# A retention-plus-MLP kernel: two loads moved behind two turns, the last product cut 192 and 64, and the first q fetched from two queues

## The chip, the cores and the metric

The kernel runs on one core of a Trainium2 chip. Its time is device microseconds of one execution; the median of three runs stands for it. Inside the core, TensorE (PE) multiplies, VectorE (DVE), ScalarE (ACT) and GpSimd (POOL) do elementwise work and copies, and SyncE (SP), ACT and POOL start DMAs.

## The reference

A retention recurrence over 4 batches, 8 heads, 768 steps and head size 64 gives `y`; its rows, heads side by side, are the 3072 tokens of an MLP with 512 inputs and 2048 hidden units and the activation `h * tanh(softplus(h))` (Mish).

```python
state = gamma * state + k_t v_t^T          # per head, gamma = 1 - 2^-(5+h)
y_t   = scale * q_t state
x     = y.transpose(0, 2, 1, 3).reshape(3072, 512)
h     = x @ w_in                            # 512 x 2048
out   = mish(h) @ w_out                     # 2048 x 512
```

## The kernel before

The recurrence is done in chunks of 128 steps: inside a chunk a masked score product `k q` and its product with `v`, across chunks a 64x64 state per head. There are 24 chunks. They are gathered into blocks of tokens for the MLP: block 0 holds four chunks, and blocks 1 to 10 two chunks each. For a block of two chunks both matrix products are done by a seven-product scheme on 2x2 parts (sums of parts are formed on DVE, seven products run on PE, and the results are added up), so their accumulators are copied out part by part.

The order of all work is written by hand. `g1_seven` runs the first product in the order of the string `ORDER`; `seven` runs the second. Between the products stand named steps (`at1`, `m1`, `m2`, ...), and `steps_of_first(1)` and `steps_of(blk)` say what each does for the chunks of later blocks: load q and v (`load_to`, on SP), bring k (`bring_k`, on POOL's queue), scale q and v to half precision on POOL (`cast_q`, line 414, `cast_v`, line 431), turn q and k of a chunk by a DMA transpose (`turn_by_dma`, line 443, on SP), score (`scores_two`, line 509), mask, outer products and states. `store` and `store_due` send finished rows out on SP. Each engine and each queue takes its work in the order in which the program lists it.

In block 1, step `at5` stores two tiles and calls `load_to(a + 4)`, which loads q and v of chunk 11; then step `m5` turns chunk 8, and step `m2` turns chunk 9. Both turns' results are read by `scores_and_outer(9)` in block 2, which scores chunks 8 and 9 in one group of 32 small products.

At the start, `load_first_q` fetches q of the first four chunks (tile `qfirst`) in two parts of four heads, both on SP, and then k, v and the weights follow on SP. The small table of decay factors, `qvs`, comes on ACT's queue. DVE scales the first half of `qfirst` (line 257) and PE turns it (line 264); DVE and POOL share the second half. Ahead of the first turn PE does filler products on constants (`spin_wide`, `spin`, lines 457 and 452).

At the end, for the last block, `seven` does after six products: `s(4) b(1,1)` into `pe`, whose sum goes out at once (half of the columns of one row tile, 128 KB, on SP); `s(3) tm(3)` into `px`, from which two sums fill the other row tile (256 KB, on ACT's queue); and `a(0,1) b(1,0)` in two pieces of 128 columns, whose sums fill the other half of the first row tile (128 KB, on SP).

Of the kernel before, what the change touches and what calls it, by code (L numbers as in the profile page):

```python
# [10 lines left out]
FP32 = mybir.dt.float32  # L11
AF = mybir.ActivationFunctionType
ALU = mybir.AluOpType
# [3 lines left out]
def kernel(  # L17
# [9 lines left out]
    nc = tc.nc  # L27
    B, H, S, D = q.shape
    d_model, d_ff = moe_w_in.shape
    P = 128  # L30
# [4 lines left out]
    TB = 512  # L35
    CPB = TB // C
# [3 lines left out]
    first = [sum(BLOCKS[:i]) for i in range(len(BLOCKS))]  # L40
# [17 lines left out]
    def toks(c):  # L58
        return slice(c * HB, (c + 1) * HB)
# [16 lines left out]

    ctx.enter_context(tc.manual_schedule())

    qvs = cpool.tile([P, (2 + CPB + R) * H], FP32, name="qvs")
    nc.scalar.dma_start(qvs, nc.inline_tensor(qvs_np, name="qvs_c").ap())  # L80
    qs, vs = qvs[:, :H], qvs[:, H:2 * H]
# [20 lines left out]
    for c in range(2):  # L102
        t = tri_half[toks(c)]
# [6 lines left out]
    for c in range(2):  # L110
        t = tri_first[c * HB:(c + 1) * HB]
# [114 lines left out]
    def rows(blk, i):  # L226
        r = out[first[blk] * P:(first[blk] + 2) * P]
        if blk <= FIRST:
            return r[i * P:(i + 1) * P]
        return r.rearrange("(n c t) d -> c t n d", n=2, c=2)[i]  # L230
# [8 lines left out]
            store(1)  # L239

    def load_first_q():

        qf = wstage.tile([P, H, CPB, D], FP32, name="qfirst", tag="wt", bufs=4)
        for a in range(0, H, H // 2):
            nc.sync.dma_start(
                qf[:, a:a + H // 2],
                q[0, a:a + H // 2, :TB].rearrange("h (p r) d -> p h r d", r=CPB))
        return qf  # L250

    def turn_first_q(qf, half, shared=False):
        a, n = half * (H // 2), H // 2
# [672 lines left out]

    def seven(blk, steps, last, rest):
        n, hf = NFB // 2, d_model // 2
        parts = 2 if last else 1
        wide = hf // parts  # L930
        px, pe = [mmps.tile([P, hf], FP32, name="o_ps", tag="mm") for _ in range(2)]
        osb = [op.tile([P, d_model], FP32, name="osb", tag="osb") for _ in range(2)]

        def a(i, j):
            return lambda f: gts[blk, j * n + f][:, i * P:(i + 1) * P]

        def b(i, j):
# [8 lines left out]
        def pieces(o_ps):  # L946
            if isinstance(o_ps, list):
                return [(t, slice(i * wide, i * wide + wide)) for i, t in enumerate(o_ps)]
            return [(o_ps, slice(0, hf))]

        def mm(o_ps, x, w, first=False, then=None):
            for t, c in pieces(o_ps):
                for f in range(n):
                    nc.tensor.matmul(  # L954
                        t, x(f), w(f)[:, c], start=first and f == 0, stop=f == n - 1,
                        skip_group_check=True)
                if then:
                    then(t, c)

        def snap(o_ps):  # L960
            x = op.tile([P, hf], FP32, name="snap", tag="snap", bufs=4)
            for t, c in pieces(o_ps):
                nc.scalar.copy(x[:, c], t)  # L963
            return x

        def store_now(queue, i, c):
            queue.dma_start(rows(blk, i)[..., c], osb[i][:, c])

        def done(i, j, o_ps, plus=None):
            dst = osb[i][:, j * hf:(j + 1) * hf]  # L970
            for t, c in pieces(o_ps):
                if plus is None:
                    nc.scalar.copy(dst[:, c], t)
                else:
                    nc.vector.tensor_tensor(dst[:, c], t, plus[:, c], op=ALU.add)  # L975

        def step(name):
            for fn, *args in steps.get(name, ()):
                fn(*args)

        mm(px, a(0, 0), b(0, 0), True)
        m1 = snap(px)
        step("g7")
        step("m1")
        if last:
            pz = mmps.tile([P, hf], FP32, name="o_ps", tag="mm")
            mm(pz, a(1, 1), tm(4), True)
            z = snap(pz)
        rest()
        pb = [mmps.tile([P, wide], FP32, name="o_ps", tag="mm") for _ in range(parts)]  # L990
        mm(pe, s(1), tm(1), True)
        m5 = snap(pe)
        step("m5")
        mm(px, s(2), tm(2))
        u2 = snap(px)
        step("m6")
        if last:
            mm(pe, s(4), b(1, 1))
            done(0, 1, pe, u2)
            store_now(nc.sync, 0, slice(hf, d_model))  # L1000
            mm(px, s(3), tm(3))
            done(1, 1, px, m5)
            done(1, 0, px, z)
            store_now(nc.scalar, 1, slice(0, d_model))
            mm(pb, a(0, 1), b(1, 0), True)
            done(0, 0, pb, m1)
            store_now(nc.sync, 0, slice(0, hf))
            return
        mm(pb, a(0, 1), b(1, 0), True)
        done(0, 0, pb[0], m1)  # L1010
        step("m2")
        mm(px, s(3), tm(3))
        done(1, 1, px, m5)
        step("m7")
        if blk > TURN:
            mm(px, a(1, 1), tm(4))
            done(1, 0, px)
        mm(pe, s(4), b(1, 1))
        if blk > TURN:
            step("m3")  # L1020
        done(0, 1, pe, u2)
        if blk <= TURN:
            step("m3")
            mm(px, a(1, 1), tm(4))
            done(1, 0, px)
        step("m4")
        for i in range(2):
            stores.append((1 + i, rows(blk, i), osb[i]))
# [28 lines left out]
                start=bp == 0, stop=bp == NBP - 1, skip_group_check=True)  # L1057

    def first_block():
        qf = load_first_q()  # L1060
        for s in range(2):
            for nm in "kv":
                for half in range(2):
# [348 lines left out]
```

## Time and profile before

| | |
|---|---|
| median of 3 runs | 192.39 us (192.24 to 194.35) |
| profiled execution | 191.71 us |
| its span in the profile | 189.8 us |
| PE busy | 183.3 us, 97% |
| DVE busy | 156.7 us, 83% |
| ACT busy | 126.0 us, 66% |
| POOL busy | 94.7 us, 50% |
| read from and written to HBM | 27.30 MB and 6.29 MB |

Rows of a timeline read: start in us, length in us, engine, line, operation, what is written <- what is read, partitions x elements, count, and in brackets how long the engine was idle before and what ended it. `SPq` and `ACTq` rows are issues of DMAs, whose landing comes later. A row of several stretches gives, for each, its length, the busy time of each engine with the number of instructions, the TensorE clock, the DMA share and GB/s. Rows of the DMA view end with the size in KB and the median us from issue to landing. In the chain of waits, each row is a piece of the path that ended last: start, length, what.

### The profile page before, as it was taken

To read this page: it belongs to the slowest core of one execution; us is meant where nothing else is said; L and a number is where in the kernel's file an instruction comes from. 1 tells how busy PE (TensorE), PEld (TensorE's weight loads), DVE (VectorE), ACT (ScalarE), POOL (GpSimd) and SP (SyncE) were. 2 spreads that over 40 slices of the span, in tenths; PEclk is the share of its full clock that TensorE was granted. 3 is DMA by queue.
4 is the path that set the end of the run, shared out by engine and by line. 5 is a ranking of instruction groups with operands and counts; after the bars stand their busy time and mean duration, and the time that the engine had idled before them with its cause. 6 is when DMAs were issued, how large, how long until landed. Compare 5 with 4: busy or idle time off the path is not lost.

```text
span 189.8 us, 7746 instructions
## 1 busy us (share of the span) xinstructions
PE 183.3 (97%) x3298; PEld 156.9 (83%) x3298; DVE 156.7 (83%) x330; ACT 126.0 (66%) x244; POOL 94.7 (50%) x135
## 2 busy tenths in 40 slices
PE   6989999999999999999999999999999999999992
PEld 2667546875988988988988988988988988989981
DVE  3997899889899698797897897797897897796662
ACT  3362699463893983894883883983884974975960
POOL 6570205696767937934934935915925923000000
PEclk9999999999999999999999999999999999999999
DMA  4999999999999999999996996996997953300203
GB/s 165 351 369 406 405 406 279 269 217 147 186 195 281 193 264 217 175 192 170 176 184 148 159 176 196 207 233 40 196 205 106 155 152 60 114 3 12 102 0 111
DMA packets 95521, 36.17 MB, mean 191 GB/s; under 512 B 82560, under 2 KB 88960, under 8 KB 95488
## 3 DMA queue, kind: packets, MB, share of 16 engines
q1 hardware_dynamic: 74112, 32.78, 73.7%
q0 software_dynamic: 21088, 2.62, 21.7%
q8 instruction: 25, 0.41, 0.9%
q10 hardware_dynamic: 288, 0.30, 0.4%
q14 instruction: 8, 0.07, 0.1%
HBM read 27.30 MB, written 6.29 MB: 177 GB/s over the span
## 4 chain that ended last, share of the span: by engine, by line
PE 94%; DVE 3%; issue 1%; POOL 0%; ACT 0%; POOLq 0%; DVEq 0%
PE h_ps L818 34%; PE o_ps L954 32%; PE h_ps L687 6%; PE o_ps L1207 5%; PE at L457 2%; PE h_ps L1055 2%; PE o_ps L1267 2%; PE y_ps L542 2%; PE at L509 2%; PE u_ps L495 2%; DVE am L329 2%; PE y_ps L553 2%; PE t_ps L264 1%; DVE osb L975 1%; PE at L322 0%
## 5 line engine op out<-in xcount | busy, mean ns | idle before, releaser
L838 DVE TENSOR_TENSOR hsum<-h_ps,hsnap 128x512 f32<-128x512 f32 x60 | 38.6, 685 | 9.7 <-ACT hsnap L828 6.8
L828 ACT COPY hsnap<-h_ps 128x512 f32<-128x512 f32 x60 | 32.1, 589 | 10.0 <-PE h_ps L818 9.7
L818 PEld LDWEIGHTS <-wsum 128*128 128x128 f16 x640 | 36.2, 98 | 0.2
L833 ACT ACTIVATE g<-hsum 128x512 f16<-128x512 f32 x60 | 34.6, 642 | 0.6 <-DVE hsum L838 0.2
L954 PEld LDWEIGHTS <-gsum 128*128 128x128 f16 x320 | 30.4, 98 | 3.7
L818 PE MATMUL h_ps<-xsum,wsum 128*128 128x128 f16 x480 | 30.2, 219 | 0.0
L954 PE MATMUL o_ps<-tmat,gsum 128*128 128x256 f16 x240 | 29.5, 273 | 0.0
L818 PEld LDWEIGHTS <-win 128*128 128x128 f16 x480 | 28.2, 98 | 0.9
L426 POOL DMA_DIRECT2D qk<-in_k_dram x36 | 27.6, 781 | 0.0
L954 PEld LDWEIGHTS <-g 128*128 128x128 f16 x248 | 22.7, 98 | 2.5
L414 POOL TENSOR_TENSOR qk<-qf,qvs 128x512 f16<-128x512 f32 x20 | 21.5, 1077 | 0.2 <-issue 0.2
L431 POOL TENSOR_TENSOR v<-vf,qvs 128x512 f16<-128x512 f32 x20 | 21.2, 1085 | 0.0
L954 PE MATMUL o_ps<-wout,g 128*128 128x256 f16 (+1 forms) x168 | 20.8, 267 | 0.0
L818 PE MATMUL h_ps<-xt,win 128*128 128x128 f16 x320 | 19.6, 219 | 0.0
L603 POOL TENSOR_TENSOR stc<-suc,gcv 128x256 f16<-128x256 f32 x15 | 9.9, 663 | 15.7 <-DVE suc L598 15.7
L560 ACT COPY hsum<-y_ps 128x512 f32<-128x512 f32 x9 | 5.3, 585 | 18.4 <-PE y_ps L553 18.4
L975 DVE TENSOR_TENSOR osb<-o_ps,snap 128x256 f32<-128x256 f32 (+1 forms) x32 | 13.0, 413 | 5.0 <-PE o_ps L954 2.5
L439 POOL COPY gate<-gsum 128x1 f16<-128x1 f16 x10 | 1.8, 185 | 26.8 <-DVE gsum L925 26.8
L963 ACT COPY snap<-o_ps 128x256 f32<-128x256 f32 x31 | 11.4, 371 | 5.5 <-PE o_ps L954 5.3
L818 PE MATMUL h_ps<-xsum,win 128*128 128x128 f16 x160 | 12.3, 220 | 0.0
L818 PE MATMUL h_ps<-xt,wsum 128*128 128x128 f16 x160 | 12.2, 219 | 0.0
L833 ACT ACTIVATE g<-h_ps 128x512 f16<-128x512 f32 x20 | 12.0, 598 | 0.0
(142 smaller groups left out, 310.6 us busy)
## 6 DMA issues: line engine op xcount, KB each, us to landing
vf<-in_v_dram SPq DMA_DIRECT2D x24, 256.0 KB, 6.0
out_dram<-osb SPq DMA_DIRECT2D x22, 256.0 KB, 3.5
qf<-in_q_dram SPq DMA_DIRECT2D x20, 256.0 KB, 4.9
wi<-in_moe_w_in_dram SPq DMA_DIRECT2D x3, 1024.0 KB, 10.5
wt<-in_moe_w_out_dram SPq DMA_DIRECT2D x3, 1024.0 KB, 9.3
qk<-in_k_dram POOLq DMA_DIRECT2D x36, 64.0 KB, 4.7
qfirst<-in_q_dram SPq DMA_DIRECT2D x2, 512.0 KB, 4.3
kf<-in_k_dram SPq DMA_DIRECT2D x4, 256.0 KB, 5.0
```

Of the source, the lines that this page charges most:

```text
L414: nc.gpsimd.tensor_tensor(by_head(g, room16(g)[0]), by_head(0, loaded[g][0]), f.broadcast_to((P, 2, HP, D)), op=ALU.mult)
L426: nc.gpsimd.dma_start(room16(g)[1][:, x::2], src[:, HP * x:HP * x + HP])
L431: nc.gpsimd.tensor_tensor(room16(g)[2], loaded[g][2], vs.unsqueeze(2).broadcast_to((P, H, D)), op=ALU.mult)
L603: by.tensor_tensor(stcs[g], sus.pop(g), decay, op=ALU.mult)
L687: nc.tensor.matmul(h_ps[:, j], win(s, f, bp), xt(blk, bp), start=(bp == 0), stop=(bp == NBP - 1))
L818: nc.tensor.matmul(h_ps[g][:, f], w(g, f, d), x(d), start=first and f == 0 and d == 0, stop=d == n - 1, skip_group_check=True)
L828: nc.scalar.copy(x, h_ps)
L833: nc.scalar.activation(gt[:, fb:fb + FPS, j * P:(j + 1) * P], h, AF.Mish, scale=inv_boost3)
L838: nc.vector.tensor_tensor(h, h_ps, x, op=ALU.add)
L954: nc.tensor.matmul(t, x(f), w(f)[:, c], start=first and f == 0, stop=f == n - 1, skip_group_check=True)
L963: nc.scalar.copy(x[:, c], t)
L975: nc.vector.tensor_tensor(dst[:, c], t, plus[:, c], op=ALU.add)
```

## The change

Three edits, independent of each other. The first q is loaded at the very beginning of the program in three parts: heads 2 and 3 on ACT's queue ahead of `qvs`, heads 0 and 1 on SP, then heads 4 to 7 on SP. In block 1, `load_to(a + 4)` moves from step `at5` to step `m2`, behind the turn of chunk 9. In the last block, `a(0,1) b(1,0)` is cut into 192 columns ahead of the last two products and 64 columns behind them, these two change places, and the stores become 256 KB on ACT, 224 KB and 32 KB on SP. On PE, DVE, ACT and POOL nothing else moves; on SP all else keeps its order.

```diff
+    qf = wstage.tile([P, H, CPB, D], FP32, name="qfirst", tag="wt", bufs=4)
+    for queue, h0, n in ((nc.scalar, 2, 2), (nc.sync, 0, 2), (nc.sync, 4, 4)):
+        queue.dma_start(
+            qf[:, h0:h0 + n],
+            q[0, h0:h0 + n, :TB].rearrange("h (p r) d -> p h r d", r=CPB))
     qvs = cpool.tile([P, (2 + CPB + R) * H], FP32, name="qvs")
     nc.scalar.dma_start(qvs, nc.inline_tensor(qvs_np, name="qvs_c").ap())
...
-    def load_first_q():
-
-        qf = wstage.tile([P, H, CPB, D], FP32, name="qfirst", tag="wt", bufs=4)
-        for a in range(0, H, H // 2):
-            nc.sync.dma_start(
-                qf[:, a:a + H // 2],
-                q[0, a:a + H // 2, :TB].rearrange("h (p r) d -> p h r d", r=CPB))
-        return qf
...
     def seven(blk, steps, last, rest):
         n, hf = NFB // 2, d_model // 2
-        parts = 2 if last else 1
-        wide = hf // parts
+        near = D
...
         if last:
-            mm(pe, s(4), b(1, 1))
-            done(0, 1, pe, u2)
-            store_now(nc.sync, 0, slice(hf, d_model))
+            def left(c):
+                pb = mmps.tile([P, c.stop - c.start], FP32, name="o_ps", tag="mm")
+                mm(pb, a(0, 1), b(1, 0), True, c)
+                done(0, 0, pb, m1, c)
+
+            left(slice(near, hf))
             mm(px, s(3), tm(3))
             done(1, 1, px, m5)
             done(1, 0, px, z)
             store_now(nc.scalar, 1, slice(0, d_model))
-            mm(pb, a(0, 1), b(1, 0), True)
-            done(0, 0, pb, m1)
-            store_now(nc.sync, 0, slice(0, hf))
+            mm(pe, s(4), b(1, 1))
+            done(0, 1, pe, u2)
+            store_now(nc.sync, 0, slice(near, d_model))
+            left(slice(0, near))
+            store_now(nc.sync, 0, slice(0, near))
             return
...
     def first_block():
-        qf = load_first_q()
...
-            "at5": [(store, 2), (load_to, a + 4), (sums_a, blk, A)],
+            "at5": [(store, 2), (sums_a, blk, A)],
...
             "m2": [(sums_c, blk), (gate_s, blk), (cast_q, a + 1), (turn_by_dma, a + 1),
-                   (store, 2)],
+                   (load_to, a + 4), (store, 2)],
```

More of the change, by code (lines that the diff above doesn't have):

```diff
@@ L944, in tm, with mm @@
             return lambda f: tmats[(i - 1) // 2][:, (i - 1) % 2, f]
[L946 to L958, printed above, removed]
+        def mm(o_ps, x, w, first=False, c=slice(0, hf)):
+            for f in range(n):
+                nc.tensor.matmul(
+                    o_ps, x(f), w(f)[:, c], start=first and f == 0, stop=f == n - 1,
+                    skip_group_check=True)
         def snap(o_ps):
             x = op.tile([P, hf], FP32, name="snap", tag="snap", bufs=4)
-            for t, c in pieces(o_ps):
-                nc.scalar.copy(x[:, c], t)
+            nc.scalar.copy(x, o_ps)
             return x
@@ L967, in store_now, with done @@
             queue.dma_start(rows(blk, i)[..., c], osb[i][:, c])
[L969 to L975, printed above, removed]
+        def done(i, j, o_ps, plus=None, c=slice(0, hf)):
+            dst = osb[i][:, j * hf:(j + 1) * hf][:, c]
+            if plus is None:
+                nc.scalar.copy(dst, o_ps)
+            else:
+                nc.vector.tensor_tensor(dst, o_ps, plus[:, c], op=ALU.add)
         def step(name):
@@ L989, in seven @@
         rest()
-        pb = [mmps.tile([P, wide], FP32, name="o_ps", tag="mm") for _ in range(parts)]
+        if not last:
+            pb = mmps.tile([P, hf], FP32, name="o_ps", tag="mm")
         mm(pe, s(1), tm(1), True)
@@ L1004, in seven @@
             store_now(nc.scalar, 1, slice(0, d_model))
-            mm(pb, a(0, 1), b(1, 0), True)
-            done(0, 0, pb, m1)
-            store_now(nc.sync, 0, slice(0, hf))
+            mm(pe, s(4), b(1, 1))
[3 more added lines that the diff above has]
+            store_now(nc.sync, 0, slice(0, near))
             return
         mm(pb, a(0, 1), b(1, 0), True)
-        done(0, 0, pb[0], m1)
+        done(0, 0, pb, m1)
         step("m2")
```

## The prediction

> **What bounds the kernel now.** I read the page first, then the chain of work that ended last, then the stretches of the three places that the change touches. The page's head and its chain shares say that TensorE is the bound nearly everywhere:
>
> ```profile
> span 189.8 us, 7746 instructions
> PE 183.3 (97%) x3298; PEld 156.9 (83%) x3298; DVE 156.7 (83%) x330; ACT 126.0 (66%) x244; POOL 94.7 (50%) x135
> ...
> PE 94%; DVE 3%; issue 1%; POOL 0%; ACT 0%; POOLq 0%; DVEq 0%
> ```
>
> The profiled execution took 191.71 us: a span of 189.8 and 1.9 around it. The three runs have their median at 192.39, 0.68 above it. So a load, a store or a turn matters only where PE waits for it, at the start before PE is saturated, or after PE's last product. The chain in order of time gives those places (start, length, what):
>
> ```profile
> 6.50 0.85 PE t_ps L264 x8
> ...
> 8.45 0.24 PE t_ps L307 x4
> ...
> 68.64 0.13 PE at L509 x16
> 68.77 0.02 issue
> 68.78 0.32 PE at L509 x16
> ...
> 185.30 1.19 DVE osb L975 x4
> ```
>
> The reader is to see a chain that is PE almost without a break, one seam at 68.77 in the middle of a group of score products, and a tail that is DVE and then the store.
>
> **The moved loads.** The seam first. The busy time of line 509 alone, for the 32 score products of two successive blocks:
>
> ```profile
> 68.46:69.03 0.57, 0.55 (x32) 0.40 (x32) 1.00 1.35 212
> 82.77:83.34 0.57, 0.37 (x32) 0.26 (x32) 1.00 1.65 196
> ```
>
> The same 32 products stretch over 0.55 us in the block that scores chunks 8 and 9 and over 0.37 in the next: PE loses about 0.18 us between chunk 8's 16 and chunk 9's. The issue queues before it, and then the landing of the second transpose alone:
>
> ```profile
> 57.81 1.03 POOL L414 TENSOR_TENSOR qk<-qf,qvs 128x512 f16<-128x512 f32 x1
> 58.76 0.45 SPq L155 DMA_DIRECT2D qf<-in_q_dram  x1
> 59.26 0.83 SPq L155 DMA_DIRECT2D vf<-in_v_dram  x1
> 59.66 1.04 POOL L414 TENSOR_TENSOR qk<-qf,qvs 128x512 f16<-128x512 f32 x1
> 60.27 2.98 SPq L443 DMA_TRANSPOSE qkt<-qk  x1
> 63.42 1.23 SPq L443 DMA_TRANSPOSE qkt<-qk  x1
> ```
>
> ```profile
> DMA to landing us min/median/max: 5.3/5.3/5.3
> ```
>
> 63.42 + 5.3 = 68.7: chunk 9's turn lands just when PE goes on at 68.78. That turn is what PE waits for. The change takes two issues (0.45 + 0.83 us of SP, 256 KB each) from before the two turns to behind the second. The first turn's q is scaled at 57.81 + 1.03 = 58.84, so it can be issued at about 58.9 instead of 60.27, 1.4 us earlier. The second, whose q is ready at 60.70, stays behind the first turn's 2.98 us of issue and goes at about 62.0 instead of 63.42. Its data also no longer stands behind 512 KB of chunk 11 in the queue. It lands at 67.4 at the latest, with 1.2 us to spare before 68.6. The gain in this execution is therefore the stall and nothing more: -0.18 us. Since the landing sits on the very edge, an execution in which it is later loses more there, and the median is 0.68 above the profiled one; bounds for the runs are 0.18 to 0.18 + 0.68 = 0.86, and I take 0.4, between the two and nearer the one row that shows it.
>
> What is late next: chunk 11's v and q. They are issued at about 63.3 and 63.8. The page's medians from issue to landing, and the first use, the scaling of v:
>
> ```profile
> vf<-in_v_dram SPq DMA_DIRECT2D x24, 256.0 KB, 6.0
> ...
> qf<-in_q_dram SPq DMA_DIRECT2D x20, 256.0 KB, 4.9
> ```
>
> ```profile
> 71.86 1.03 POOL L431 TENSOR_TENSOR v<-vf,qvs 128x512 f16<-128x512 f32 x1
> ```
>
> So both are there by 69.8, and 2 us are left. Behind the moved loads on SP stand two stores and chunk 12's loads; SP does the same total work up to there, and no engine waits for the stores. I cost the delay at nothing; without that margin, POOL's scaling and the state products behind it would slip one for one.
>
> **The first q.** Today two 512 KB parts come one behind the other on SP, and the small table `qvs` (32 KB) on ACT's queue. Afterwards ACT's queue brings heads 2 and 3 and only then `qvs`; SP brings heads 0 and 1 and then heads 4 to 7. The second half keeps its place: the same bytes are ahead of it.
>
> ```profile
> 0.74 1.00 SPq L247 DMA_DIRECT2D qfirst<-in_q_dram  x2
> 4.69 2.02 DVE L257 TENSOR_TENSOR qfirst<-qfirst,qvs 128x1024 f16<-128x1024 f32 x2 [1.80 <-DMA qfirst<-in_q_dram]
> 5.44 1.06 PE L452 MATMUL at<-ident 128*128 128x512 f16 x2
> 5.97 0.10 PEld L264 LDWEIGHTS <-qfirst 128*128 128x128 f16 x1 [0.37 <-DVE qfirst L257]
> 6.14 1.49 POOL L257 TENSOR_TENSOR qfirst<-qfirst,qvs 128x512 f16<-128x512 f32 x1 [1.98 <-DMA qfirst<-in_q_dram]
> 6.29 1.06 PE L264 MATMUL t_ps<-ident,qfirst 128*128 128x128 f16 x8
> ```
>
> DVE indeed waits 1.80 us for the first half. But PE is then in its filler products on `tri` and `ident`, which stand ahead of the transposes in its own order. The two on `ident` start at 5.44 and the transposes follow at 6.29 without a gap, while their weights could be loaded at 5.97. An earlier q moves DVE's cast, not the transposes: gain 0 in this execution. A later q costs only beyond the slack of about 0.2 us (5.97 against 6.29, less one weight load of 0.10). How fast the first bytes come (0.2 us a slice, from the start):
>
> ```profile
> GB/s 0 0 0 0 0 0 0 0 9 146 33 41 148 68 164 374 333 389 389 389 379 379 394 374 389 389 374 351 353 340 356 338 348 340 346 341 340 353 343 343
> ```
>
> From 1.8 to 3.0 the queue runs at about 100 GB/s, and from 3.0 at 370. If that slow stretch belongs to one queue, two of them shorten it; at best the whole 1.2 us less 0.3 for its bytes, 0.9. If it belongs to the engines, nothing changes, and `qvs`, now behind 256 KB, lands with the q instead of ahead of it. [...] I take 0, with -0.3 to +1.1 as bounds (both under the rivals).
>
> **The last product.** The order s(4)·b, s(3)·t, then 128 and 128 columns becomes 192 columns, s(3)·t, s(4)·b, then 64 columns; the stores, 128 KB early, 256 and 128 KB late, become 256 KB on ACT, 224 KB and 32 KB on SP, all late.
>
> ```profile
> 183.35 1.04 PE L954 MATMUL o_ps<-wout,gsum 128*128 128x256 f16 x8
> 183.55 0.37 ACT L963 COPY snap<-o_ps 128x256 f32<-128x256 f32 x1 [0.50 <-PE o_ps L954]
> 184.23 1.04 PE L954 MATMUL o_ps<-tmat,gsum 128*128 128x256 f16 x8
> 184.49 0.42 DVE L975 TENSOR_TENSOR osb<-o_ps,snap 128x256 f32<-128x256 f32 x1 [1.20 <-PE o_ps L954]
> 184.94 0.54 SPq L967 DMA_DIRECT2D out_dram<-osb  x1
> 185.30 1.19 DVE L975 TENSOR_TENSOR osb<-o_ps,snap 128x256 f32<-128x256 f32 x4 [0.39 <-PE o_ps L954]
> 185.97 0.51 DVE L975 TENSOR_TENSOR osb<-o_ps,snap 128x128 f32<-128x128 f32 x2
> 186.09 0.65 ACTq L967 DMA_DIRECT2D out_dram<-osb  x1
> 186.51 0.54 SPq L967 DMA_DIRECT2D out_dram<-osb  x1
> ```
>
> ```profile
> out_dram<-osb SPq DMA_DIRECT2D x1, 128.0 KB, 2.0
> ...
> out_dram<-osb SPq DMA_DIRECT2D x1, 128.0 KB, 2.4
> ...
> qvs<-qvs_c ACTq DMA_DIRECT2D x1, 32.0 KB, 2.4
> ```
>
> Eight products of 256 columns take 184.23 - 183.35 = 0.88 us, so 192 columns take 0.66: from 183.35, s(3) starts at 184.01 and s(4) at 184.89, and it ends at 185.77. s(3) writes where ACT still copies u2; that copy ends at 183.55 + 0.37 = 183.92, so the shorter product ahead of it leaves 0.09 us where there was 0.31, and no stall. DVE begins 0.26 behind a group's end (184.23 to 184.49). So ACT's store goes 0.22 earlier than its 186.09, at about 185.9. The sum of s(4) runs 186.03 to 186.45, and the 224 KB store is issued at 186.48. No row has 64 columns over 128 rows: eight cost between a quarter of 0.88, 0.22, and eight times the 0.06 of the chain's four transposes of 128 columns, 0.48. Either way PE ends by 186.25 and the last sum, at most 0.25 long, by 186.75. This decides nothing, because SP is busy with the 224 KB issue until 186.48 + 0.54 = 187.02. The last store, 32 KB, is issued at about 187.07, where the last one is issued at 186.51 now and lands 2.4 later, at 188.9. The unknown is its landing. Upper bound: the only 32 KB transfer took 2.4, giving 189.5, +0.6. Lower bound: the small store is free and the 224 KB one ends the kernel, 186.48 + 2.4 = 188.9, 0. I take 2.0, the row of a 128 KB store with nothing ahead of it: 189.1, +0.2.
>
> **Sum** against the profiled execution: -0.18 + 0 + 0.2 = 0.0, so 191.7. Against the runs, with 0.4 for the stall: 192.39 - 0.4 + 0.2 = 192.2.
>
> **Rivals.** (1) The runs lose more at the turn than the profiled execution, and the head helps as well. For: the landing is on the edge, the runs are slower than the profile, and full PE speed comes only between the chain's transposes at 6.50 (0.106 each) and those at 8.45 (0.06). An execution in which it came two microseconds earlier would save some 0.4 on the eight transposes and would then wait for POOL's quarter of q, so that earlier bytes count, up to the 0.3 above. [...] Against: no row shows such a run. Time: 192.39 - 0.86 + 0.2 = 191.7, or 191.4 with the head.
>
> (2) Slower, by the tail: the last store waits on SP behind the 224 KB issue and its 256-byte rows land no faster than the 2.4 of `qvs`. It decides as soon as the last sum is ready before 187.02. Time: 192.39 - 0.18 + 0.6 = 192.8. [...] Against: 32 KB is little, and nothing stands behind it.
>
> (3) Slower, by the head: `qvs` or heads 2 and 3 come out of ACT's queue only with SP's second half, whose wait on POOL ended at 6.1. DVE would start at 6.1 instead of 4.69 and the transposes about 7.4 instead of 6.29: +1.1. It decides from 0.2 us of lateness. For: `qvs` is queued behind 256 KB and both casts read it. Against: 32 KB on that queue landed 2.4 after its issue beside SP's load, so ACT's queue is not starved. Time: 192.2 + 1.1 = 193.3.
>
> (4) The turns don't land earlier, because the transposes are limited by something other than the two loads. Time: 192.39 + 0.2 = 192.6. Against: 512 KB at the 212 GB/s of line 509's stretch is 2.5 us of queue.
>
> **How the numbers follow.** Forecast, no change: 0.55. Rival 1: 0.20. Rival 2: 0.12. Rival 3: 0.10. Rival 4: 0.03. The time is 192.2. The range 191.4 to 193.4 takes in rival 1 with the head's gain and rival 3's price. A measurement of this kernel tells about 1% from no change, that is 190.5 and 194.3. None of the cases reaches 190.5; I leave 0.04 for a stall that no row shows. Rival 3 with a later rise of PE's speed on top could pass 194.3; with other surprises 0.06. Within 1%: 0.90.
>
> **What would show it.** Right: line 509's products of chunks 8 and 9 in about 0.37 us and no seam there; the second turn issued before 62.5; POOL's scaling of chunk 11's v not later than now; the first transposes directly behind the filler products; SP's two last issues back to back, the last at about 187 counted on the old scale, with a landing 2.0 behind. Wrong: a gap on PE ahead of the first transposes (rival 3), DVE waiting for `qvs`, a new wait on POOL near 72, or a last landing clearly before the old one, relative to PE's last product.

## The result, and the profile after

The changed kernel is slower: 194.91 us (median of 22 runs) against 192.97 for the kernel before (22 runs beside them), a ratio of 1.0072 with a 95% interval of 1.0048 to 1.0096, or 1.4 us (0.9 to 1.9). The ratio leaves out the seven slowest of the 22 runs, six of which show a low granted PE clock (more below); the median is that of all 22.

The first profiled execution of the changed kernel is one of these six (197.18 us). From its page, the span, the busy time and the granted PE clock in 40 slices of 4.9 us (in tenths; a 6 is a slice mostly at half speed):

```profile
span 195.4 us, 7749 instructions
PE 185.9 (95%) x3298; PEld 158.3 (81%) x3298; DVE 158.8 (81%) x330; ACT 126.6 (65%) x244; POOL 95.2 (49%) x135
PEclk9966999999999999999999999999999999999999
```

The third and fourth slices run at reduced speed. The granted clock in stretches of two microseconds (length, busy PE, clock, DMA share, GB/s):

```profile
8.00:10.00 2.00, 1.17 (x16) 1.00 1.15 345
10.00:12.00 2.00, 1.20 (x18) 0.81 1.13 357
12.00:14.00 2.00, 2.00 (x37) 0.50 1.09 387
16.00:18.00 2.00, 2.00 (x37) 0.50 1.07 414
18.00:20.00 2.00, 2.00 (x34) 0.98 1.03 392
```

Half speed begins within 10 to 12 (0.81 is 0.38 of the stretch at half, so at 11.24) and ends at 18.07. Before it, PE is busy for only 1.2 of 2 us. Why it idles, from the chain in order of time and from PE's timeline:

```profile
1.26 4.46 DMA qvs<-qvs_c
...
5.85 2.69 DVE qfirst L253 x2
8.54 2.41 DVE qk L287 x2
```

```profile
5.44 1.06 PE L448 MATMUL at<-ident 128*128 128x512 f16 x2
7.13 0.93 PE L260 MATMUL t_ps<-ident,qfirst 128*128 128x128 f16 x8 [0.63 <-DVE qfirst L253]
...
8.59 0.62 PE L260 MATMUL t_ps<-ident,qfirst 128*128 128x128 f16 x8 [0.26 <-DVE qfirst L253]
9.79 0.40 PE L303 MATMUL t_ps<-ident,qk 128*128 128x128 f16 x4 [0.58 <-DVE qk L287]
10.99 0.42 PE L303 MATMUL t_ps<-ident,qk 128*128 128x128 f16 x4 [0.80 <-DVE qk L287]
```

The table `qvs` lands at 1.26 + 4.46 = 5.72, where it landed at 3.1 before. Heads 0 to 3, which the two queues share, are there earlier than before (issue to landing 3.2 and 3.5 us in the rows below, against 3.8 before), but DVE's scaling needs `qvs` as well and starts at 5.85 instead of 4.69. These are single executions: in seven profiles with the head of before DVE starts at 4.69 to 5.28, in seven with the new one at 5.39 to 5.85. The reader is to see four gaps on PE, of 0.26 to 0.80 us; in the same stretch the kernel before has one, of 0.17:

```profile
7.68 0.77 PE L264 MATMUL t_ps<-ident,qfirst 128*128 128x128 f16 x8
8.29 0.61 PE L307 MATMUL t_ps<-ident,qk 128*128 128x128 f16 x8
8.74 0.44 PE L457 MATMUL at<-tri 128*128 128x128 f32 x2
9.35 0.42 PE L322 MATMUL at<-qfirst_t,qkt 64*64 64x128 f16 x16 [0.17 <-ACT qkt L312]
```

The DMAs of the changed kernel:

```profile
qfirst<-in_q_dram ACTq DMA_DIRECT2D x1, 256.0 KB, 3.5
qfirst<-in_q_dram SPq DMA_DIRECT2D x1, 256.0 KB, 3.2
...
qvs<-qvs_c ACTq DMA_DIRECT2D x1, 32.0 KB, 4.5
out_dram<-osb SPq DMA_DIRECT2D x1, 32.0 KB, 2.0
```

A second profile of the same kernel (run changed_again below) caught an execution whose clock did not fall. The two beside the kernel before, by milestones (starts in us; in brackets what the stretch since the milestone above lost or gained against before):

| | before | second profile | first profile |
|---|---|---|---|
| first product of the MLP | 15.15 | 15.45 (+0.30) | 19.24 (+4.09) |
| scores of chunks 6 and 7 | 54.39 | 54.49 (-0.20) | 58.27 (-0.21) |
| scores of chunks 8 and 9 | 68.47 | 68.54 (-0.03) | 73.38 (+1.03) |
| scores of chunks 10 and 11 | 82.70 | 82.57 (-0.20) | 87.43 (-0.18) |
| last group of scores | 166.77 | 166.65 (+0.01) | 171.51 (+0.01) |
| last store lands | 188.87 | 188.98 (+0.23) | 193.84 (+0.23) |
| end of the span | 189.80 | 190.55 (+0.64) | 195.40 (+0.63) |

So the loss stands at four places: the head (0.3, or 4.1 with the clock), one wait in the middle that one execution has and the other not, the last store (0.23), and 0.63 behind the last landing, where nothing is computed any more. The middle gains 0.2 at the place of the moved loads, and 0.2 of the head's loss is already made up before the scores of chunks 6 and 7.

### The profile page after: what moved, and what is told of

It is laid out like the page before. It is cut to its first block, busy times and chain, and to the rows that moved or that the text cites. A ratio compares the mean times of both kernels' runs of the same rounds, so it can differ in the third digit from the quotient of the medians.

```text
span 195.4 us, 7749 instructions
## 1 busy us (share of the span) xinstructions
PE 185.9 (95%) x3298; PEld 158.3 (81%) x3298; DVE 158.8 (81%) x330; ACT 126.6 (65%) x244; POOL 95.2 (49%) x135
## 4 chain that ended last, share of the span: by engine, by line
PE 80%; DMA 8%; POOL 4%; DVE 3%; issue 1%; ACT 1%; ACTq 0%; DVEq 0%; SPq 0%; POOLq 0%
PE o_ps L943 31%; PE h_ps L814 30%; PE h_ps L683 5%; DMA qk<-in_k_dram 3%; DMA qvs<-qvs_c 2%; DMA qkt<-qk 2%; PE h_ps L1046 2%; POOL v L427 2%; PE y_ps L538 2%; PE at L505 2%; PE y_ps L549 1%; PE u_ps L491 1%; DVE qfirst L253 1%; POOL qk L410 1%; DVE qk L287 1%; POOL qk L422 1%
## 5 line engine op out<-in xcount | busy, mean ns | idle before, releaser
L943 PE MATMUL o_ps<-wout,g 128*128 128x256 f16 (+2 forms) x168 | 20.9, 268 | 0.0
L960 DVE TENSOR_TENSOR osb<-o_ps,snap 128x256 f32<-128x256 f32 (+2 forms) x32 | 13.1, 414 | 5.8 <-PE o_ps L943 3.1
```

Of the source, the lines that this page charges most:

```text
L943: nc.tensor.matmul(o_ps, x(f), w(f)[:, c], start=first and f == 0, stop=f == n - 1, skip_group_check=True)
L960: nc.vector.tensor_tensor(dst, o_ps, plus[:, c], op=ALU.add)
```

## The experiments

Each run below was compared with the kernel before on the same chip. The theory (H) was that the head is the cost, because `qvs` stands behind 256 KB on ACT's queue; its rivals put the cost in the tail (T) or in the moved loads (L).

**One edit at a time.** head_alone, loads_alone and tail_alone are the kernel before with one of the three edits.

```diff
 head_alone:  + for queue, h0, n in ((nc.scalar, 2, 2), (nc.sync, 0, 2), (nc.sync, 4, 4)): ...   (ahead of qvs)
 loads_alone: "m2": [..., (turn_by_dma, a + 1), + (load_to, a + 4), (store, 2)]
 tail_alone:  + left(slice(near, hf)); mm(px, ...); mm(pe, ...); left(slice(0, near))
```

> The kernel before with the first q from two queues as its only edit. Theory H (the head is the cost: the table qvs stands behind 256 KB on ACT's queue and lands at 5.7 us instead of 3.1, so DVE's first scaling starts at about 5.85 instead of 4.69): 1.1 to 1.4 us slower than the kernel before, gaps on PE ahead of the first turns. Theory T (the tail is the cost): within 0.3 us of the kernel before. Theory L (the moved loads are the cost): within 0.3 us.

Measured: 1.0063 (1.0021 to 1.0106), 1.2 us. First product of the MLP at 16.13, and the gaps on PE. H holds as far as the head's edit is the main cost. Not all of it is lateness: in this profile the end comes 1.34 us behind the last landing instead of 0.93, because the edit adds a DMA (see below).

> The kernel before with chunk 11's loads moved behind the turns as its only edit. Theory H: 0.2 to 0.4 us faster, the 32 score products of chunks 8 and 9 without a seam. Theory T: the same. Theory L: over 0.5 us slower, with a new wait in block 1 or 2.

Measured: 0.9998 (0.9963 to 1.0033). L falls. The gain is too small for this interval; it was run again below.

> The kernel before with the last product as 192 and 64 columns and the stores of 256, 224 and 32 KB as its only edit. Theory H: 0.2 us slower by the last landing, up to 0.8 with the time from the last landing to the end, which was 1.56 us in the changed kernel's profile and 0.93 in that of before. Theory T: 1.2 us slower or more. Theory L: within 0.3 us.

Measured: 1.0024 (0.9987 to 1.0062). T falls as the main cost. The trace shows the last landing 0.25 later, counted from the first of the last three products, and 0.2 more behind it.

**Is it the place of `qvs`, or the split?**

```diff
 qvs_first:    qvs on ACT's queue ahead of heads 2 and 3
-    nc.scalar.dma_start(qvs, ...)         # behind the parts of q
+    nc.scalar.dma_start(qvs, ...)         # ahead of them
 qvs_on_sp:    + nc.sync.dma_start(qvs, ...)     # first on SP, heads 0 and 1 behind it
 qvs_on_pool:  + nc.gpsimd.dma_start(qvs, ...)   # POOL's queue, behind the making of tri
```

> The changed kernel with qvs put back ahead of heads 2 and 3 on ACT's queue; all else as changed. Theory H: qvs lands at about 3.1 us, DVE's first scaling starts at 4.6 to 5.0, and 1.0 us or more of the loss comes back: within 0.5 us of the kernel before. Rival H2 (the cost is the split of q over two queues, not the place of qvs): heads 2 and 3 land at 5.5 or later, DVE starts as late as in the changed kernel, and the loss of 1.4 us stays. Theories T and L: the loss stays as well, though DVE starts early.

Measured: 1.0217 (1.0158 to 1.0275); the median is 4.7 us above the kernel before, that of the changed kernel 1.9. Four of the six runs have a granted clock of 0.990 or less, and the profile shows the fall (10.93 to 17.76), so the clock has a part in this. Now `qvs` lands at 2.8, and heads 2 and 3, which stand second on ACT's queue, are the late ones, as the chain shows (1.18 + 4.53 = 5.71):

```profile
1.18 4.53 DMA qfirst<-in_q_dram
5.71 0.03 issue
5.74 0.05 DVEq L253
5.79 0.05 issue
5.84 2.69 DVE qfirst L253 x2
```

H in its first form, that the place of `qvs` is the cost, falls: in both orders what stands second on ACT's queue lands late, at 5.3 to 5.8, 0.05 to 0.6 us ahead of SP's second half (5.88 here, 5.77 in the changed kernel).

> The changed kernel with qvs as the first transfer of SP's queue, ahead of heads 0 and 1; ACT's queue brings heads 2 and 3 alone. Theory H3 (what stands second on ACT's queue shares the DMA engines with SP's second half and lands with it, at 5.3 to 5.8 us, whichever transfer it is): with one transfer on ACT there is no second one, so qvs lands at about 3 us and heads 0 to 3 by 4.7, DVE's first scaling starts at 4.3 to 4.8, and the time is within 0.6 us of the kernel before. Rival H2 (two queues at once are slow for the first half in any order): heads 0 and 1 or heads 2 and 3 land at 5.3 or later, and the loss of 1.2 to 1.4 us stays.

Measured: 1.0133 (1.0086 to 1.018), 2.6 us, where 0.6 at most was expected. The landings came as H3 says (`qvs` 2.9, heads 0 to 3 by 4.3), and DVE starts earlier than before. But SP's second half is 1.5 us later than before, and the gain turns into a larger wait:

```profile
4.45 1.22 DVE L253 TENSOR_TENSOR qfirst<-qfirst,qvs 128x1024 f16<-128x1024 f32 x1 [1.57 <-DMA qfirst<-in_q_dram]
7.56 0.69 DVE L253 TENSOR_TENSOR qfirst<-qfirst,qvs 128x512 f16<-128x512 f32 x1 [1.88 <-DMA qfirst<-in_q_dram]
```

Its transfers between 4 and 5 us, in half microseconds, and below them those of the changed kernel (last column, GB/s):

```profile
4.00:4.50 0.50, 0.50 (x1) 1.00 0.92 154
4.50:5.00 0.50, 0.50 (x2) 1.00 0.65 219
```

```profile
4.00:4.50 0.50, 0.50 (x1) 1.00 1.12 385
4.50:5.00 0.50, 0.50 (x2) 1.00 1.09 367
```

One DMA more stands ahead of that half on SP, so that it is issued at 1.71 instead of 1.26; that this starves the queue was not shown.

> The changed kernel with qvs on POOL's queue, behind POOL's making of tri. Theory H3 (what stands second on a queue beside SP's second half lands with it): with nothing second on ACT's queue, heads 0 to 3 land by 4.3 us and SP's stream is as in the changed kernel (second half at 5.8); if qvs, issued at about 1.9, lands by 4.6, DVE starts at 4.3 to 4.7 and the head is as early as before or 0.2 us earlier. Rival: a third queue shares as well, qvs lands at 5 us or later, and DVE starts later than before; then 0.4 us or more of the head's loss stays.

Measured: 1.0246 (1.02 to 1.0292). The rival holds: issued at 1.77, `qvs` takes 4.85 on the third queue and lands at 6.6, later than anywhere else; heads 0 to 3 are there by 4.2 and wait for it. In each of the four arrangements that fetch q from two queues something that DVE's first two operations need comes late: `qvs`, heads 2 and 3, or the second half.

**Why DVE takes so long, and why PE's clock falls.**

DVE's two casts of k, in the kernel before, in the two profiles of the changed kernel, and in v_by_dve (ns of one: least, median, most):

```profile
L291 DVE CAST qk<-kf x2: 415/775/1135, 6.8 to 7.8; 128x512 f16<-128x512 f32 x2
```

```profile
L287 DVE CAST qk<-kf x2: 1276/1276/1276, 8.5 to 9.7; 128x512 f16<-128x512 f32 x2
```

```profile
L287 DVE CAST qk<-kf x2: 415/415/415, 8.0 to 8.3; 128x512 f16<-128x512 f32 x2
```

```profile
L287 DVE CAST qk<-kf x2: 414/415/416, 8.0 to 8.3; 128x512 f16<-128x512 f32 x2
```

One and the same cast takes 0.42 us or up to 1.28. In all 19 profiles (38 casts) it takes 0.98 to 1.28 where an operation of POOL is under way when it starts, and ends some 0.3 us behind that operation; it takes 0.41 to 0.42 where none is, even if POOL's next one starts during it. The kernel before has one long cast (beside POOL's part of q), the first profile of the changed kernel two (beside the scaling of v), the second none, head_alone one.

```diff
 v_by_dve (cast_two):
-            nc.gpsimd.tensor_tensor(
+            (nc.vector if s == 0 else nc.gpsimd).tensor_tensor(
```

> The changed kernel with the first two scalings of v on DVE instead of POOL, so that POOL has nothing to do while DVE casts k. Theory D (POOL's operation makes DVE wait: 0.42 us for a cast of k alone, 1.28 beside POOL's scaling): both casts of k 0.40 to 0.45 us, the two turns of k within 0.6 us of each other and the second by 9.6 us (10.99 in the first profile of the changed kernel, 9.7 in three others), and no run with a granted clock under 0.99. The two scalings take DVE about 1.4 us later on, ahead of the second mask, so the time is 0.5 us below the changed kernel's fast runs to 0.8 above them, that is 0.9 to 2.2 us above the kernel before. Rival (the casts are long for another reason, as k arriving late): casts of 1.0 us or more stay, and clocks under 0.99 too.

Measured: 1.0245 (1.0208 to 1.0281). The casts and turns came as theory D says: with POOL idle both casts take 0.415, and both turns of k start on PE at 8.6. The second profile of the changed kernel has the same casts without this edit, so it is the 38 casts taken together that show POOL to be what makes them long. The time came out far above the expectation, for the same reason one step later: now two scalings of v stand on DVE beside POOL's next ones and take 1.4 and 1.5 us (in the kernel before DVE's scaling of q in the same shape, begun while POOL was idle, took 0.69), and PE waits for them.

```profile
11.34 2.84 DVE L292 TENSOR_TENSOR v<-vf,qvs 128x512 f16<-128x512 f32 x2
```

```profile
12.78 0.61 PE L337 MATMUL u_ps<-v,qk 64*128 64x128 f16 x8 [1.60 <-DVE v L292]
14.23 0.61 PE L337 MATMUL u_ps<-v,qk 64*128 64x128 f16 x8 [0.85 <-DVE v L292]
```

Its granted clock was 0.991 or less in all six runs. I had forecast none: the gaps were not removed but moved.

```diff
 filled, and qvs_first_filled on top of qvs_first:
         spin(at, 8)
+        spin(at, 4)          # ahead of the first turns of q
+        spin(at, 8)          # ahead of turn_two(0, 0), and again of turn_two(0, 1)
```

> The changed kernel with filler products on PE in three of its gaps at the start: 512 columns ahead of the first turns of q, 1024 columns ahead of each of the first two turns of k. Theory C (the clock falls back to half speed in some runs because PE idles 0.6 to 0.8 us at a time between 6.5 and 11 us): no run with a granted clock under 0.99, first product of the MLP at 16.0 to 16.5 us, runs 1.2 to 1.8 us above the kernel before and none 4 us above. Rival: the clock falls for another reason; then a third of the runs lie 3 to 5 us above the kernel before, as for the changed kernel.

> The kernel with qvs ahead of heads 2 and 3 on ACT's queue, with the same filler products in PE's gaps as in the filled one. Theory C (idle PE between 6.5 and 11 us lets the granted clock fall back): four of six runs of the kernel without filler had a granted clock of 0.979 to 0.99; here at most one in six is below 0.993, and the time falls from 4 us to 1.3 to 2.0 us above the kernel before. Rival: the clock depends on something else and half of the runs or more stay below 0.993.

Measured: filled 1.0079 (1.0045 to 1.0112), first product of the MLP at 16.31; qvs_first_filled 1.0106 (1.0058 to 1.0154). Runs with a low granted clock:

| kernel | 0.991 or less | 0.985 or less |
|---|---|---|
| before, beside the experiments | 0 of 115 | 0 |
| q on SP alone, with other edits (seven series) | 3 of 82 | 0 |
| changed (both series) | 11 of 28 | 6 |
| head_alone, head_and_loads, head_and_tail | 12 of 36 | 7 |
| qvs_first / with filler | 4 of 6 / 1 of 6 | 3 / 0 |
| changed with filler | 1 of 8 | 0 |
| qvs_on_sp | 0 of 6 | 0 |
| qvs_on_pool | 4 of 6 | 4 |
| v_by_dve (more gaps) | 6 of 6 | 5 |

The clock of a run is a mean over its span, and the four traces that show a fall at the start have 0.976 to 0.983. Between that and 0.991 it is open what happened, because traces without a fall at the start also have half speed at the very end, where PE has no products left (0.89 us of it in the kernel before, 2.98 in head_and_tail, with a mean of 0.992).

Theory C holds in direction: kernels with the gaps have the falls, and with filler products, which compute nothing, none of 14 runs is at 0.985 or less, against 9 of 34 of the same two kernels without. The counts are small, and it isn't complete. PE in qvs_on_sp is busy for 1.40 and 1.17 us of the 2 us from 6 and from 8, in head_alone's profile for 1.05 and 1.12, and in neither did the clock fall. Nor is every late run a fall: one of changed_again and two of head_and_tail took 197.1 to 197.6 us at a granted clock of 0.999 or more. No trace shows them; the profile of head_and_tail shows one other way to lose 2 us: last stores that take 4.0 and 4.5 us instead of 2.0 and 2.4.

**Behind the last landing.** The end of the program waits one by one for the completion lanes of the DMAs (the semaphores by which they report their landing). In the kernel before, the last store is on the lane that is waited for last; the changed kernel has one DMA more (three parts of q for two), and its last store is on a lane behind which seven more waits stand: in its first profile SP's wait for that lane stands at 193.86, those for the other seven follow from 193.92 to 194.29, 0.06 us apart, and the first DRAIN comes at 194.35. The step behind the waits, the first of the three DRAINs, before (landing 188.87) and in the second profile (landing 188.98):

```profile
L1407 SPq DRAIN  x3: 7/7/7, 189.0 to 189.3; - x3
```

```profile
L1397 SPq DRAIN  x3: 7/7/13, 189.5 to 189.8; - x3
```

```diff
 one_more_dma (kernel before, second half of q in two):
-        for a in range(0, H, H // 2):
+        for a, n in ((0, 4), (4, 2), (6, 2)):
```

> The kernel before with the second half of the first q fetched by two DMAs of two heads each, both on SP: one DMA more in the program, nothing else. Theory E (the waits at the end of the program stand in a fixed order of completion lanes; one DMA more moves the last store onto the lane that is waited for first, so that eight further waits of about 0.06 us follow its landing): from the last landing to the end of the span 1.3 to 1.6 us instead of 0.93, and 0.3 to 0.6 us slower. Rival: the time from the last landing to the end stays at 0.9 to 1.1 us, and the kernel is within 0.2 us of the one before.

Measured: 1.0046 (1.0016 to 1.0077), 0.9 us, where 0.3 to 0.6 was expected. From the last landing to the end 1.56 us, against 0.93. By the trace the first step behind the waits comes 0.51 us after the landing instead of 0.08. The same 0.51 stands in all ten profiles whose last store is on that lane (and whose last landing is recorded), and 0.08 in all eight where it is on the last one. The other 0.2 lies in the last barrier, and no edit is shown to cause it: one_more_dma has it with the old tail, v_by_dve has the new tail and not the 0.2. The last two stores of this one execution took 4.1 and 4.2 us, so only the time behind the landing is read from it.

```diff
 tail_last_on_act (tail_alone):
-            store_now(nc.sync, 0, slice(0, near))
+            store_now(nc.scalar, 0, slice(0, near))
```

> The kernel before with the changed tail, the last store of 32 KB on ACT's queue behind its 256 KB instead of on SP's behind 224 KB. Theory S (the last store waits for SP's issue of 224 KB): it is issued at about 0.5 us earlier than in the tail-only kernel (2.7 instead of 3.2 to 3.8 us behind ACT's first store's start, by the queue's own issue of 0.65), the last landing is then that of the 224 KB store, 5.6 us behind the start of the last three products instead of 5.77, against 5.52 in the kernel before. Rival: behind 256 KB on one queue the 32 KB land later than 2.0 us after their issue, and the last landing is not earlier than 5.77. By time: within 0.4 us of the kernel before under either.

Measured: 1.0061 (1.0029 to 1.0094), which neither expected. Issued 0.4 us earlier (0.76 behind ACT's first store instead of 1.18 in tail_alone), the 32 KB land 2.44 after their issue instead of 2.0, behind the 256 KB, so the last landing comes no earlier: 5.78 behind the start of the last three products, against 5.77. The rival holds. By its trace 0.2 us are lost at the head and 0.55 from there to the first scores, where the edit changes nothing, 0.26 up to the last landing and 0.2 behind it.

**Two edits at a time, and the wait in the middle.** In the first group of score products PE sometimes waits for the turn of chunk 7. Whether an edit causes this:

```diff
 head_and_loads: - the tail's edit;  loads_and_tail: - the head's edit;  head_and_tail: - the loads' edit
 loads_and_tail_2, changed_again, loads_alone_2: the same kernels again, on one chip
```

> The changed kernel with the tail of before: the first q from two queues and the moved loads. So far the four kernels that hold all edits show PE waiting 0.6 to 1.0 us for the turn of chunk 7 in the first group of score products (about 39 us behind the first product of the MLP), and none of the six that hold one edit or none of the three does; the turn's landing lies on the edge in all of them. Theory P (this wait is a matter of how the transfers of chunk 7 happen to run, and of no edit): it can come here or not, and in loads_and_tail as in head_and_tail. Theory L2 (the moved loads cause it): it comes here and in loads_and_tail, not in head_and_tail. Time: 1.0 to 1.4 us above the kernel before without the wait, 1.8 to 2.3 with it.

> The changed kernel with the head of before. No extra DMA, so the last store is on the lane that is waited for last. Sum of the single edits: -0.2 for the seam of chunks 8 and 9, +0.25 for the landing, +0.2 behind it: 0.0 to 0.5 us above the kernel before. Under theory L2 a wait of 0.6 to 1.0 us for chunk 7's turn on top, so 0.8 to 1.5; under theory P it may come or not.

> The changed kernel with chunk 11's loads where they were before. Sum of the single edits: +0.9 at the first product of the MLP, +0.25 for the landing, +0.5 to 0.7 for the waits behind it: 1.6 to 1.9 us above the kernel before, the seam of chunks 8 and 9 still there. Under theory L2 no wait for chunk 7's turn.

Measured: 1.0031 (0.9994 to 1.0067), 0.9972 (0.9942 to 1.0002) and 1.0052 (1.0013 to 1.009). The wait came in the first, not in the second, and a little in the third (0.2). The three times are 0.6 us above, 0.5 below and 1.0 above the kernel before; each is lower than was expected.

> The changed kernel, for a profile on the same chip as the three others. Sum of the single edits against the kernel before: +0.9 at the first product of the MLP (16.1 us instead of 15.2), -0.2 at chunks 8 and 9, +0.25 at the last landing, +0.6 behind it, that is 1.5, and 0.4 to 1.0 more where PE waits for chunk 7's turn. If that wait belongs to the kernel with both edits it is in this profile too (0.4 us or more); if it is chance, it need not be. With the clock fallen back (first product at 19 us), 4 us or more.

> The moved loads with the new tail and the head of before, beside the moved loads alone. By the traces the tail costs 0.25 us at the last landing and 0.2 behind it: 0.45 us above the loads alone, and 0.0 to 0.3 above the kernel before. If the tail is worth something instead, it is below the loads alone, as the first comparison of it with the kernel before (0.9972) would have it.

Measured: 1.0109 (1.0059 to 1.0158) and 1.0036 (1.0008 to 1.0064). The two intervals of loads_and_tail, one and the same kernel in two series, don't overlap (0.9942 to 1.0002 and 1.0008 to 1.0064): a few tenths of a us are read from the traces here, not from these times. This time the changed kernel has no such wait, and loads_and_tail has one, where its first profile had none. PE's waits for this turn in head_and_loads and in loads_and_tail_2 (us in total, times, longest):

```profile
PE at L505 <- DMA qkt<-qk: 0.4, 1, 0.4
```

```profile
PE at L509 <- DMA qkt<-qk: 0.3, 1, 0.3
```

So the same kernel has the wait in one execution and not in another, and L2 falls (in the kernel before, the loads that the edit moves are issued from 58.8 on, behind this wait). That no edit has a part in it, as theory P says, isn't shown: of the eleven profiles with q on two queues seven have it (0.4 to 0.9 us) and one a little (0.2), of the eight with q on SP alone one (0.3). A part of the head is an open rival. The turn lands 38.7 to 40.6 us behind the first product of the MLP, and PE needs it from 39.0 on.

> The moved loads alone. By the traces the seam between chunks 8 and 9 costs 0.1 to 0.4 us in six kernels with the loads in their old place and nothing in the others: 0.1 to 0.4 us below the kernel before. Rival: what the seam gives comes back as a wait elsewhere, and the time is that of the kernel before.

Measured: 0.9975 (0.9953 to 0.9998), 0.5 us faster than the kernel before. The busy time of line 509 for the 32 score products of chunks 8 and 9, and of the next block:

```profile
68.57:69.14 0.57, 0.43 (x32) 0.32 (x32) 1.00 1.03 203
82.60:83.17 0.57, 0.45 (x32) 0.33 (x32) 1.00 1.48 250
```

The first group is no longer the slower one. This version, the moved loads without the two other edits, has the lowest ratios of the kernels measured twice (0.9998 and 0.9975, against 0.9972 and 1.0036 for loads_and_tail); only one of the two intervals leaves out no change, and by the spread between series just seen a gain is not certain.

## Why the prediction was wrong, point by point

The forecast was 192.2 us, no change; the range ended at 193.4. The sum started from 192.39, the median of three runs; beside the changed kernel the kernel before stood at 192.97, so 0.6 us of the distance to 194.91 is in the base and not in the change.

**The moved loads: right.** The stall was put at 0.18 in the profiled execution and at 0.4 over the runs. Every kernel with the moved loads lost nothing at the seam, the kernels without lost 0.1 to 0.4, and the second profile of the changed kernel gains 0.20. The second turn was to be issued before 62.5 and was issued at 60.9. The 0.55 and 0.37 of the prediction come from windows that cut up to 0.08 us off each group; the whole groups are 0.63 and 0.45, with the same difference of 0.18. Before, and then in the second profile:

```profile
68.47 0.63 PE L509 MATMUL at<-qkt 64*64 64x64 f16 x32
82.70 0.45 PE L509 MATMUL at<-qkt 64*64 64x64 f16 x32
```

```profile
68.53:69.10 0.57, 0.43 (x32) 0.33 (x32) 1.00 0.95 221
82.56:83.13 0.57, 0.45 (x32) 0.33 (x32) 1.00 1.31 284
```

**The first q: the step that failed.** The sum took 0 with +1.1 as upper bound, and rival 3, which named the mechanism (`qvs` behind 256 KB on ACT's queue, gaps on PE ahead of the turns), got 0.10. head_alone measured 1.2 us (0.4 to 2.0) for the step put at 0. The argument against rival 3 was a row of the trace: 32 KB on ACT's queue landed in 2.4 beside SP's load. That row was of a transfer with nothing ahead of it, in the stretch in which SP itself moved little (about 100 GB/s from 1.8 to 3.0); it says nothing of a transfer that comes second. In the runs the second one on ACT lands at 5.3 to 5.8, 0.05 to 0.6 us ahead of SP's 512 KB, and in qvs_on_pool `qvs`, alone on its queue, takes 4.85 us, against 2.1 and 2.2 where it is first on ACT's or SP's queue beside the same loads (qvs_first, qvs_on_sp). No run shows the 0 of the sum: it was the author's estimate from the filler products of one execution.

Rival 3 had the lateness nearly right (DVE at 6.1; measured 5.39 to 5.85), and its +1.1 lies close to the 1.2 of head_alone, but that is luck: it moved the casts as blocks, and the price is made up of other things. DVE's casts met other operations of POOL and took 0.42 to 1.28 us each, none, one or both of them long (one was long before). The 38 casts are long (0.98 to 1.28) where an operation of POOL was under way as they began, short (0.41 to 0.42) elsewhere. And with the gaps PE's clock falls in some runs (6 of 28 by the stricter count, 11 by the wider), which costs some 3 us at once (19.24 against 16.1 for the first product). Without a fall the first product is 0.3 to 1.0 us late by the traces (15.45 to 16.13, against a mean of 15.15 in seven profiles with the old head, which lie between 14.8 and 15.4).

Most of that lateness doesn't last. From the first product to the scores of chunks 6 and 7 the second profile, head_alone, head_and_loads and head_and_tail need 39.0 us, the seven profiles with the old head 39.2 to 40.2, so that these scores start at 54.5 to 55.2 (mean 54.98) against 54.4 to 55.4 (mean 54.78). Why the old head loses more in this stretch stays open. What stays of the edit is the fall of the clock, the 0.43 us at the end that its additional DMA brings (0.51 instead of 0.08), and perhaps the wait for chunk 7.

Rival 1's execution, in which PE is fast earlier and waits for POOL's part of q, does occur, with the old head (loads_alone and tail_alone, first product at 14.88 and 14.80, a wait of 0.52); no profile shows the new head gaining from it.

**The last product: right in its working, incomplete at the end.** Issue times and landings, in the second profile of the changed kernel:

```profile
183.24 0.82 PE L943 MATMUL o_ps<-wout,g 128*128 128x192 f16 x8
...
185.64 0.40 PE L943 MATMUL o_ps<-wout,g 128*128 128x64 f16 x8
185.81 0.63 ACTq L953 DMA_DIRECT2D out_dram<-osb  x1
186.37 1.20 SPq L953 DMA_DIRECT2D out_dram<-osb  x2
```

On the old scale (0.11 later) ACT's store goes at 185.92 (forecast 185.9) and SP's at 186.48 and 187.11 (186.48 and 187.07); the last one lands 2.0 behind its issue, so that the landing is 0.23 later (forecast 0.2). What was missed is that the end of the program is not the last landing: 1.56 us follow it instead of 0.93; 0.43 of the difference are the waits and 0.2 the barrier. No term of the sum stood for that, because the change was not seen to touch it. The additional DMA is the head's, so this too belongs to the step put at 0.

**The sum.** Against the 1.4 us of the ratio the traces give the head 0.3 to 1.0 at the first product, the last store 0.23, the end 0.63 and the seam -0.2: 1.0 to 1.7. What is made up before the scores of chunks 6 and 7 would lower this, the wait for chunk 7 (0 to 0.9) raise it, so the shares are not settled: the second profile's span is only 0.75 longer than before. Of the 15 runs behind the ratio three have a granted clock of 0.987 to 0.991; the mean of the other twelve is 0.9 us above that of the kernel before (without its one run at 196.71).

The upper end of the range (193.4) was built from rival 3 alone and left out that the rivals add up. A later rise of PE's speed on top of rival 3 was named, but outside the range, and a fall of the clock is none of its cases.

## What to carry to other kernels

Before a transfer is put ahead of a small table that every first operation reads, ask when the table lands beside everything issued so far (here its 32 KB took 4.0 to 4.85 us second on ACT's queue or on POOL's, and 2.1 to 3.0 first on ACT's or SP's); a row of a transfer with nothing ahead of it is no evidence. At the start of a kernel price a delay by what it newly puts side by side (here a cast on DVE took 0.42 us, or up to 1.28 beside POOL) and by PE's idle share (here a fall of the clock cost some 3 us in 6 of 28 runs), not only as a shift, and read whether the shift is still there at a later milestone. And read what lies between the last landing and the end of the span: here one DMA more at the start moved the last store to another lane, and the step behind the waits came 0.43 us later.

## What the runs showed of the hardware that was not expected

- Two queues at once, with q first on both, brought the first 512 KB 0.3 to 0.9 us earlier (4.25 in the changed kernel against 4.59 to 5.18 in seven profiles), but the second transfer on the short queue ended at most 0.6 us ahead of the long queue's: 32 KB took 4.0 to 4.5 us from issue to landing there (changed_again, first profile), and 2.1 to 3.0 where they were first on a queue (qvs_first 2.1, qvs_on_sp 2.2, the kernel before 2.4, loads_alone_2 3.0).
- A cast of 128x512 from single to half precision on DVE took 0.41 to 0.42 us where no operation of POOL was under way when it started, and 0.98 to 1.28 us where one was (38 of 38 casts).
- PE at 1.2 busy of 2 us lost half its clock from 11.24 to 18.07, 6.83 us, in one execution of the changed kernel; in its second profile, at 1.55 to 1.88 busy of 2 us from 6 to 12, it did not. The fall of qvs_first (10.93 to 17.76) lasts 6.83 us as well, that of v_by_dve 6.8 by its clock of 0.60 from 12 to 14 and 0.69 from 18 to 20, and the 0.982 of qvs_on_pool over its 194.2 us is 7.0 at half speed. Why it lasts so long, and why only some runs of a kernel show it, was not shown.
- The waits at the end of the program cost about 0.06 us each and run in the order of the lanes: the step behind them came 0.51 us behind the last landing where seven more waits follow that lane's (the expectation of one_more_dma has eight), 0.08 where it is the last.
